# Two blocks of two feed-forward networks side by side, three of their products by quarters: seven products for eight

## The chip, the core and the metric

The kernel runs on one core of a Trainium2 chip. Its engines work in parallel: TensorE (PE, with its weight loads shown apart as PEld), VectorE (DVE), ScalarE (ACT), GpSimd (POOL) and SyncE (SP, which issues transfers). The metric is the device time of one launch in microseconds; three runs of the kernel before took 807.57, 808.49 and 808.75 us, a median of 808.49.

## What is computed

Attention over 16 heads of 768 rows (with a mask by hashed buckets), then two feed-forward networks on the 1536 rows it gives:

```python
attn_out = _attn_ref(**attn_kwargs)                       # (2, 8, 768, 64)
x = np.ascontiguousarray(attn_out.transpose(0, 2, 1, 3)).reshape(B * S, H * D)   # (1536, 512)

def _moe_ref(x, w_in, w_out):                             # w_in 512 x 2048, w_out 2048 x 512
    h = x @ w_in
    sp = np.where(h > 20.0, h, np.log1p(np.exp(np.minimum(h, 20.0))))
    return ((h * np.tanh(sp)) @ w_out).astype(np.float32)

def _moe2_ref(x, w1, w2, w3, w_out):                      # w1, w2 512 x 1024, w3 1024 x 1024, w_out 1024 x 512
    a = x @ w1
    b = x @ w2
    return ((a * b @ w3) @ w_out).astype(np.float32)
```

## The kernel before, in words

The 1536 rows are three blocks of 512 (`TB`). Block 0 goes through both networks while attention is still running for the heads of the second half (`ff_first`); blocks 1 and 2 follow when attention is done. The product of w3 and the last w_out is made once (`wprod`), so the second network is two products a and b, their elementwise product, and one more matrix product.

To reach float32 accuracy with a fast matrix format, every operand is cut in a high part and a residue (`split`, L698 on ScalarE and L700 on VectorE), and each product is three matmuls: high by high, high by residue, residue by high (`PASS`). A matmul has a 128 by 128 weight tile and up to 512 moving columns.

For blocks 1 and 2 the functions are, in the order of the work: `b_h` (one group of the first layer, 256 features: 2 halves x 4 contraction tiles x 3 passes = 24 matmuls of 512 columns on an s tile of two PSUM banks, L812 in `h_ops`; then Mish on ScalarE, L1144, and the cut into two parts, L1147 and L1149), `b_out` (the second layer, 24 matmuls of 512 columns, L1166, accumulating over all 8 groups in the four b banks), `b_x2` (cuts its result), `b_ab` (128 features of a and of b, again 24 matmuls of 512 columns on an s tile, L1193; a copy L1201, a multiplication L1202, a cut L1204 and L1205) and `b_o` (the last product, 12 matmuls a step, L1221, accumulating over 8 steps in the four b banks). Block 1 runs from its first layer to its output, then block 2; `step_list` writes out this order with a few groups of the next block moved forward. The weights are fetched from device memory for each block again (`wt`, `fetch`, L691).

The engines' orders are not written by hand. Every operation is given to `Plan.op` with its engine, an assumed cost, what it reads and writes, and a due time; `Plan.run` then plays the program forward and lets each engine take the ready operation with the earliest due time for which a buffer is free. Buffers come from pools (`Val(pool, kind, limit)`): K8 are 8 KB tiles, named k in the trace, F4 4 KB tiles, named f; PSUM has eight banks, four in two s tiles (SP_) and four b tiles (BP). Numbers in `CFG` are due times and limits. At the place called `swap` the attention's SBUF tiles are given back and the pools K8 and F4 grow.

## Time and profile before

| | us |
|---|---|
| median of 3 runs | 808.49 |
| the profiled execution, its own time | 809.2 |
| span of that execution, first to last instruction | 807.1 |
| TensorE busy | 791.4 |
| VectorE busy | 563.2 |
| ScalarE busy | 450.9 |
| GpSimd busy | 89.9 |

The span is what the instruction rows cover; the profiled execution's own time has 2.1 us more around it. Busy is the time in which at least one instruction of the engine was running by its record. A matmul's record is longer than the spacing of matmuls, because they are pipelined, so the spacing is read from starts, not from durations.

### The profile page before, as it was taken

The numbers are of one execution on the slowest core, as the hardware profiler recorded it, in microseconds if no ns is written. First come the engines' busy times: TensorE is split into PE (matmuls) and PEld (weight loads), VectorE is DVE, ScalarE is ACT, GpSimd is POOL, SyncE is SP. The second block draws the span as 40 slices with busy tenths as digits, with TensorE's granted clock in tenths as the row PEclk, the third lists the DMA queues.
The fourth block names the chain that finished last, engine by engine and source line by source line (L and its number), as shares of the span: only waits on it lengthen the run. The fifth ranks groups of instructions, "written<-read, shape, count | busy, mean of one in ns | idle before, by whom it ended". The sixth has DMA issues, their size and how long they took to land.

```text
span 807.1 us, 10733 instructions
## 1 busy us (share of the span) xinstructions
PE 791.4 (98%) x3995; PEld 621.3 (77%) x3995; DVE 563.2 (70%) x803; ACT 450.9 (56%) x724; POOL 89.9 (11%) x154
## 2 busy tenths in 40 slices
PE   8999899999999999999999999999999999999998
PEld 7667789887676777677777778888888888888886
DVE  6999799999998899999997666633733353233412
ACT  4897657668879776885774434533342254323311
POOL 4111011011221131221311100000000000000000
PEclk9999999999999999999999999999999999999999
DMA  7665446385765585847654436823122208300001
GB/s 222 206 226 184 140 140 199 95 283 162 228 232 181 199 261 169 303 146 249 176 215 163 159 108 222 300 74 96 66 79 90 94 18 321 104 27 0 1 1 52
DMA packets 42603, 124.90 MB, mean 155 GB/s; under 512 B 5156, under 2 KB 11652, under 8 KB 41528
## 3 DMA queue, kind: packets, MB, share of 16 engines
q1 hardware_dynamic: 26152, 59.08, 23.5%
q0 software_dynamic: 16256, 65.02, 22.7%
q8 instruction: 31, 0.51, 0.3%
q14 instruction: 20, 0.16, 0.1%
q10 hardware_dynamic: 144, 0.13, 0.0%
HBM read 94.37 MB, written 17.87 MB: 139 GB/s over the span
## 4 chain that ended last, share of the span: by engine, by line
PE 84%; DVE 10%; ACT 3%; issue 2%; DMA 1%; DVEq 0%; ACTq 0%; SPq 0%
PE s L1193 11%; PE b L1166 11%; PE s L812 11%; PE b L828 8%; PE b L610 6%; PE s L527 6%; PE b L581 6%; PE b L1221 5%; PE b L923 5%; PE b L812 5%; PE b L748 4%; DVE st L536 2%; PE s L471 2%; PE s L500 1%; DVE f L651 1%
## 5 line engine op out<-in xcount | busy, mean ns | idle before, releaser
L700 DVE TENSOR_TENSOR k<-f,k 128x1024 fp32r<-128x1024 f32 x96 | 115.9, 1219 | 73.7 <-ACT k L698 73.6
L539 ACT ACTIVATE E<-s,st 128x768 f32<-128x768 f32 x96 | 87.0, 906 | 37.6 <-DVE st L536 29.5
L698 ACT CAST k<-f 128x1024 fp32r<-128x1024 f32 x96 | 98.7, 1047 | 9.7 <-PE b L828 7.0
L536 DVE TENSOR_REDUCE st<-s 128x1 f32<-128x768 f32 x96 | 91.0, 950 | 9.0 <-PE s L527 8.6
L581 PE MATMUL b<-ident,E 128*128 128x128 f32 x576 | 91.9, 275 | 1.0 <-DVE k L630 0.8
L581 PEld LDWEIGHTS b<-ident,E 128*128 128x128 f32 x576 | 70.7, 140 | 27.0 <-issue 7.2
L1193 PE MATMUL s<-k,k 128*128 128x512 f32 x384 | 91.1, 393 | 0.0
L1166 PE MATMUL b<-k,k 128*128 128x512 f32 x384 | 90.0, 392 | 0.0
L812 PE MATMUL s<-k,k 128*128 128x512 f32 x384 | 90.0, 391 | 0.0
L1193 PEld LDWEIGHTS s<-k,k 128*128 128x128 f32 x384 | 72.1, 188 | 16.7
L1166 PEld LDWEIGHTS b<-k,k 128*128 128x128 f32 x384 | 72.2, 188 | 16.2
L812 PEld LDWEIGHTS s<-k,k 128*128 128x128 f32 x384 | 72.2, 188 | 15.9
L828 PE MATMUL b<-k,k 128*128 128x512 f32 x288 | 78.4, 406 | 0.8 <-ACT f L858 0.8
L828 PEld LDWEIGHTS b<-k,k 128*128 128x128 f32 x288 | 50.8, 188 | 17.5 <-issue 7.8
L610 PE MATMUL b<-T,v 128*64 128x384 f32 x288 | 62.0, 511 | 0.4 <-ACT T L405 0.3
L1202 DVE TENSOR_TENSOR f<-s,f 128x512 f32<-128x512 f32 x16 | 11.1, 692 | 69.4 <-ACT f L1201 69.4
L527 PE MATMUL s<-kb,qb 128*128 128x384 f32 x192 | 55.3, 369 | 2.3 <-DVE qa L507 1.3
L1144 ACT ACTIVATE f<-s 128x1024 f32<-128x1024 f32 x16 | 16.4, 1028 | 73.1 <-PE s L812 73.1
L748 PE MATMUL b<-k,k 128*128 128x512 f32 x192 | 53.3, 413 | 2.4 <-ACT T L405 2.0
L812 PE MATMUL b<-k,k 128*128 128x512 f32 x192 | 53.8, 408 | 0.0
L1201 ACT COPY f<-s 128x512 f32<-128x512 f32 x16 | 9.4, 587 | 76.7 <-PE s L1193 76.7
L405 ACT COPY T<-b 128x384 f32<-128x384 f32 x85 | 39.2, 479 | 20.4 <-PE b L581 19.8
(128 smaller groups left out, 1263.4 us busy)
## 6 DMA issues: line engine op xcount, KB each, us to landing
k<-in_moe_w_dram POOLq DMA_DIRECT2D x16, 1024.0 KB, 7.2
k<-in_moe_w_out_dram POOLq DMA_DIRECT2D x12, 1024.0 KB, 7.3
k<-in_moe_w_in_dram POOLq DMA_DIRECT2D x8, 1024.0 KB, 6.4
f<-keep_wi SPq DMA_DIRECT2D x16, 512.0 KB
f<-keep_wo SPq DMA_DIRECT2D x16, 512.0 KB
keep_wi<-f POOLq DMA_DIRECT2D x8, 512.0 KB, 3.7
f<-keep_wi POOLq DMA_DIRECT2D x8, 512.0 KB, 5.2
keep_wo<-f POOLq DMA_DIRECT2D x8, 512.0 KB, 4.6
```

The costliest lines, as they stand in the source:

```text
L527: nc.tensor.matmul(t()[:, a, 0:HS], lhsT=l()[0:kk, i * 128:(i + 1) * 128], rhs=r()[0:kk, a * HS:(a + 1) * HS], start=(l is qb), stop=(l is ...
L536: P.op("DVE", 0.868, lambda: nc.vector.tensor_reduce(out=s()[:, 0, i:i + 1], in_=t()[:, :, 0:HS], axis=AX.XY, op=ALU.max, negate=True), r= ...
L539: P.op("ACT", act(S, acc=True) + 0.11, lambda: nc.scalar.activation(out=e().rearrange("p (a n) -> p a n", a=2), in_=t()[:, :, 0:HS], func= ...
L581: nc.tensor.transpose(t()[:, ci * 128:(ci + 1) * 128], es[ci]()[:, kt * 128:(kt + 1) * 128], ident)
L610: nc.tensor.matmul(t()[r, 0:HS], lhsT=w, rhs=f(), start=first and j == 0, stop=last and j == CH - 1)
L698: P.op("ACT", act(1024, True), lambda: nc.scalar.copy(out=hl()[:, 0:1024], in_=f()), r=[f], w=[(hl, 0)], due=due, name="hi")
L700: P.op("DVE", dve(1024), lambda: nc.vector.tensor_sub(out=hl()[:, 1024:2048], in0=f(), in1=hl()[:, 0:1024]), r=[f, (hl, 0)], w=[(hl, 1)], ...
L748: nc.tensor.matmul(acc(), lhsT=hv()[:, ws, g_, :], rhs=wview(wo2[g_ // 2], 2)[:, rs, g_ % 2, :], start=(n == 0), stop=(n == 3 * GT - 1))
L812: nc.tensor.matmul(of(), lhsT=wview(w, KD)[:, ws, kk, (f % 2) * 128:(f % 2) * 128 + 128], rhs=kview(xhl[n][kk // 2], xs, kk), start=(m == ...
L828: nc.tensor.matmul(of(), lhsT=l(), rhs=rr(), start=(m == 0), stop=(m == len(ops) - 1))
L1166: nc.tensor.matmul(t(), lhsT=wview(w, 2)[:, ws, f, dd * 128:(dd + 1) * 128], rhs=gv[:, gs, f, :], start=(j == 0 and f == 0 and s == 0), st ...
L1193: nc.tensor.matmul(t()[:, x, :], lhsT=wview(w, KD)[:, ws, kk, (f % 2) * 128:(f % 2) * 128 + 128], rhs=kview(xx[kk // 2], xs, kk), start=(k ...
```

## The change

Blocks 1 and 2 run side by side, a group of block 2 behind the same group of block 1, so that a weight tile is fetched, cut and summed once for both (all but the second layer's, which is fetched for each). Their first layer and their pair a, b are computed by quarters. A group is a two by two arrangement: two halves of the contraction (256 each) and two halves of the outputs (128 features each, or a and b) against two halves of the 512 rows. Eight products of quarters would be needed; seven are made, of sums and differences of quarters of the weights (`sums`, L893) and of the rows (`quarters`, L828), and sums of their results (`add`, L934, and copies out of PSUM, L928 and L939) give the four output quarters. Each of the seven products is two contraction tiles by three passes: six matmuls of 256 columns (L906). Two PSUM banks of a new pool Q are used for a group, q0 and q1 in the code; the four banks of the attention's s tiles become these banks at `swap`, which now waits only for the operations that use attention's own pools. The last product of block 2 is not accumulated step by step in four banks but made at the end, one row tile of 128 rows after the other, the last one in two halves of 256 columns (`b_o_rows`).

```diff
     "lag": 1.92,
-    "prep": 11.92,
-    "wp0": 16.62,
+    "prep": 11.76,
+    "wp0": 16.6,
     "wp1": 42.29,
-    "dec0": 39.11,
-    "dec1": 130,
-    "ff0": 54.95,
-    "ff1": 106.09,
+    "dec0": 39.06,
+    "dec1": 124.72,
+    "ff0": 55.14,
+    "ff1": 118.67,
     "slack": 0.10,
     "k8": 12,
     "f4": 7,
     "hl": 3,
-    "F": 3,
+    "hl2": 6,
+    "sl": 2,
+    "lag2": 1,
+    "lag3": 1,
+    "hlk": 2,
+    "ahead": 13.19,
+    "clk": 190.46,
+    "g2": 3,
+    "F": 2,
     "cold": 8.0,
...
+    def quarters(xt, i, due, keep_):
...
+        sub(2, 1, 0, ["k0"], "t1", 0.3)
+        cut(0, ["k0", "t1"], 2 * NH_, 0.4)
+        sub(5, 4, 2, ["k1", "t1"], "t2", 0.5)
+        sub(6, 4, 1, ["k0", "k1"], "t3", 0.5)
+        sub(7, 3, 5, ["k1", "t2"], "t4", 0.6)
+        cut(1, ["k1", "t2", "t3", "t4"], 5 * NH_, 0.7)
...
+    def sums(view, due, name, r, n=128):
+
+        f, hl = Val(F4, "S", 1), Val(K8, "sl", CFG["sl"], FR)
+        sv = lambda x: f().rearrange("p (r i c) -> p r i c", r=4, i=2)[:, x]
+        for x, op, a, b in ((0, "add", (1, 0), (1, 1)), (1, "subtract", 0, (0, 0)), (2, "subtract", (0, 0), (1, 0)),
+                            (3, "subtract", (0, 1), 1)):
+            av = (lambda a=a: sv(a)) if isinstance(a, int) else (lambda a=a: view(*a))
+            bv = (lambda b=b: sv(b)) if isinstance(b, int) else (lambda b=b: view(*b))
+            rr = [(f, y) for y in (a, b) if isinstance(y, int)]
+            P.op("DVE", 0.335, lambda x=x, op=op, av=av, bv=bv: nc.vector.tensor_tensor(
+                out=sv(x), in0=av(), in1=bv(), op=getattr(ALU, op)), r=r + rr, w=[(f, x)], due=due, name=name)
+        split(f, hl, due + 0.5)
...
+    def seven(xs, wa_, ws_, r, due, step, done, name):
+
+        q0, q1, sx = Val(Q, "q"), Val(Q, "q"), Val(F4, "sx", 2)
+
+        def mm(q, c, lhs, o, first):
+            n = 0
+            for i in range(2):
+                for w, x in PASS:
+                    nc.tensor.matmul(q()[:, c * NH_:(c + 1) * NH_], lhsT=lhs(w, i), rhs=xs[i][x]()[:, qcol(o)],
+                                     start=first and n == 0, stop=n == 5, skip_group_check=True)
+                    n += 1
+
+        A = lambda m, h: (lambda w, i: wa_(m, h, w, i))
+        SS = lambda x: (lambda w, i: ws_(x, w, i))
+        g0 = [(v_, 0) for t in (0, 1) for v_ in xs[t]]
+        g1 = [(v_, 1) for t in (0, 1) for v_ in xs[t]]
+
+        def st1():
+            mm(q0, 0, A(0, 0), 0, True)
+            mm(q0, 1, SS(0), 2, False)
+
+        def st2():
+            mm(q1, 0, A(0, 1), 3, True)
+            mm(q1, 1, A(1, 1), 7, False)
+
+        def st3():
+            mm(q0, 0, SS(1), 5, False)
+            mm(q0, 1, SS(3), 4, False)
+
+        P.op("PE", 12 * 0.1185, st1, r=r + g0, w=[q0], due=due, name=name)
+        P.op("ACT", act(2 * NH_), lambda: nc.scalar.copy(out=sx()[:, 0:2 * NH_], in_=q0()), r=[q0], w=[(sx, 1)],
+             due=due + step, name="s1")
+        P.op("PE", 12 * 0.1185, st2, r=r + g1, w=[q1], due=due + step, name=name)
+        P.op("PE", 12 * 0.1185, st3, r=r + g1, w=[q0], due=due + 2 * step, name=name)
+
+        def add(o, q, c, x, w, dd):
+            P.op("DVE", dve(NH_), lambda: nc.vector.tensor_add(
+                out=done()[:, o * NH_:(o + 1) * NH_], in0=q()[:, c * NH_:(c + 1) * NH_], in1=sx()[:, x * NH_:(x + 1) * NH_]),
+                r=[q, (sx, w)], w=[(done, o)], due=due + dd * step, name="cc")
+
+        def get(x, w, dd):
+            P.op("ACT", act(NH_), lambda: nc.scalar.copy(out=sx()[:, x * NH_:(x + 1) * NH_], in_=q0()[:, 0:NH_]), r=[q0],
+                 w=[(sx, w)], due=due + dd * step, name="s2")
+
+        add(0, q1, 0, 0, 1, 2)
+        get(2, 2, 3)
+        add(1, q0, 1, 2, 2, 3)
+        P.op("PE", 6 * 0.1185, lambda: mm(q0, 0, SS(2), 6, False), r=r + g1, w=[q0], due=due + 3.5 * step, name=name)
+        get(3, 3, 4)
+        add(3, q0, 0, 1, 1, 4)
+        add(2, q1, 1, 3, 3, 4)
...
+    theirs = (SP_, EP, TP, QB, KB, QA, KA, XF, RW, HL, VP, TM, VS, RT, ST)
+    gate2 = P.op("SWAP", 0.01, swap, due=0, after=[x for x in P.units if any(v_.pool in theirs for v_ in x.vals)], name="swap")
...
+        lag, ahead = CFG["lag2"], CFG["hlk"]
+        for j in range(FP + ahead):
+            if j < FP:
+                prog.append(("h", 1, j))
+            if 0 <= j - lag < FP:
+                prog.append(("h", 2, j - lag))
+            if j == 0:
+                prog.append(("x", 2))
+            if j - ahead >= 0:
+                prog.append(("out", 1, j - ahead))
+        for j in range(FP + ahead - lag, FP):
+            prog.append(("h", 2, j))
+        prog.append(("x2", 1))
+        for j in range(FP):
+            prog.append(("out", 2, j))
+        prog += [("ab", 1, 0), ("x2", 2), ("ab", 1, 1)]
+        lag = CFG["lag3"]
+        for f in range(GT + lag + 1):
+            if 1 < f < GT:
+                prog.append(("ab", 1, f))
+            if 0 <= f - lag < GT:
+                prog.append(("ab", 2, f - lag))
+            if 0 <= f - 1 < GT:
+                prog.append(("o", 1, f - 1))
+        for t4 in range(TB // 128):
+            prog.append(("or", 2, t4))
+        return prog
...
+    def b_o_rows(n, t4):
+
+        d = clock[0]
+        last = t4 == TB // 128 - 1
+        ws = [wt("wp", n, j, d) for j in range(GT // 2)]
+        hd = DM // 2
+        cols = [slice(0, hd), slice(hd, DM)] if last else [slice(0, DM)]
+        for x, c in enumerate(cols):
+            t = Val(BP, "a")
+            for f in range(GT):
+                P.op("PE", pe(DM, 3) / len(cols), lambda t=t, f=f, c=c: o_mm(t, n, f, t4, c), r=[pp[n, f], ws[f // 2]], w=[t],
+                     due=d + 0.69 * f / len(cols) + x * 2.77, name=f"o{n}.{t4}")
+            if last:
+                o = Val(F4, "o", 4)
...
```

How the change moves instructions, at three places. Names are of tiles: q and b are PSUM banks, k and f SBUF tiles; the weights are named last; the number behind an underscore tells one use of a buffer from the next.

On TensorE, in the first layer of block 1 before: one group (L812) on bank pair s0, then a second-layer step (L1166).

```order
L812 MATMUL s0_67<-k3_2813,k2_4631 128x512 x6
L812 MATMUL s0_67<-k9_3946,k2_4631 128x512 x6
L812 MATMUL s0_67<-k3_2813,k2_4631 128x512 x6
L812 MATMUL s0_67<-k9_3946,k2_4631 128x512 x6
L1166 MATMUL b1_70<-k10_4665,k7_4644 128x512 x6
L1166 MATMUL b3_72<-k10_4665,k7_4644 128x512 x6
L1166 MATMUL b0_69<-k10_4665,k7_4644 128x512 x6
L1166 MATMUL b2_71<-k10_4665,k7_4644 128x512 x6
```

On TensorE now, in the first groups: the end of the third stage of one group (bank q2), the last six of the other group (q0), the last six of the first (q2 again), and the next group, which takes q0 over. Of each six the first is shown, and of the last two.

```order
L906 MATMUL q2_4672<-k12_4313,k1_4597 128x256
L906 MATMUL q2_4672<-k7_4216,k1_4597 128x256
L906 MATMUL q0_4633<-k6_3654,k13_4520 128x256
L906 MATMUL q0_4633<-k0_3668,k13_4520 128x256
...
L906 MATMUL q2_4672<-k6_3654,k1_4597 128x256
L906 MATMUL q2_4672<-k0_3668,k1_4597 128x256
...
L906 MATMUL q0_4766<-k17_4403,k5_4431 128x256
```

Where 24 matmuls of 512 columns stood without any read of their bank in between, banks are now read and written again within a group, with six or more matmuls of another bank in between.

On VectorE, in the stretch of a and b: before, per step a multiplication and a cut, and the residues of weight tiles (L700).

```order
L1202 TENSOR_TENSOR f_5370<-s_68,f_5370 128x512
L1205 TENSOR_TENSOR f_5379<-f_5370,f_5379 128x512
L1202 TENSOR_TENSOR f_5414<-s_67,f_5414 128x512
L1205 TENSOR_TENSOR f_5423<-f_5414,f_5423 128x512
L700 TENSOR_TENSOR k_5428<-f_5191,k_5428 128x1024
L700 TENSOR_TENSOR k_5436<-f_5199,k_5436 128x1024
```

Now, at the like place: the adds that put the quarters of the results together (L934), a sum of weight quarters (L893), the multiplication (L1358), a residue (L712) and a cut (L1361).

```order
L893 TENSOR_TENSOR f_6577<-f_6577,f_5978 128x256
L934 TENSOR_TENSOR f_6581<-q_6549,f_6562 128x256
L893 TENSOR_TENSOR f_6577<-f_5978,f_6577 128x256
L934 TENSOR_TENSOR f_6581<-q_6530,f_6562 128x256
L934 TENSOR_TENSOR f_6611<-q_6584,f_6543 128x256
L934 TENSOR_TENSOR f_6611<-q_6514,f_6543 128x256
L934 TENSOR_TENSOR f_6581<-q_6530,f_6562 128x256
L934 TENSOR_TENSOR f_6581<-q_6549,f_6562 128x256
L1358 TENSOR_TENSOR f_6581<-f_6581 128x512
L712 TENSOR_TENSOR k_6626<-f_6577,k_6626 128x1024
L1361 TENSOR_TENSOR f_6643<-f_6581,f_6643 128x512
```

The adds stand in front of the multiplication, and the work of two groups and of the weight sums is mixed in one queue.

On TensorE where attention ends, before: the last value product (L610), then 30 matmuls of L923 and 48 of L828 for block 0, then block 1 (L812).

```order
L610 MATMUL b_70<-T_4419,v_98 64x384
L923 MATMUL b_72<-k_3770,k_4367 128x512 x6
L923 MATMUL b_69<-k_3695,k_4299 128x512 x6
L923 MATMUL b_69<-k_3770,k_4299 128x512 x6
L923 MATMUL b_71<-k_3695,k_4367 128x512 x6
L923 MATMUL b_71<-k_3770,k_4367 128x512 x6
L828 MATMUL b_70<-k_4393,k_4277 128x512 x6
L828 MATMUL b_72<-k_4393,k_4277 128x512 x6
L828 MATMUL b_69<-k_4393,k_4277 128x512 x6
L828 MATMUL b_71<-k_4393,k_4277 128x512 x6
```

Now, behind the last value product (L620): 24 of L975, 48 of L1070, 24 of L975, 48 of L1070 and 48 of L975, which is 192 matmuls of block 0, and then L906.

```order
L620 MATMUL b_69<-T_4267,v_101 64x384
L975 MATMUL b_68<-k_4135,k_4092 128x512 x6
L975 MATMUL b_70<-k_4135,k_4092 128x512 x6
L975 MATMUL b_67<-k_4135,k_4092 128x512 x6
L975 MATMUL b_69<-k_4135,k_4092 128x512 x6
L1070 MATMUL b_68<-k_3958,k_4260 128x512 x6
L1070 MATMUL b_68<-k_3971,k_4260 128x512 x6
L1070 MATMUL b_70<-k_3958,k_4278 128x512 x6
L1070 MATMUL b_70<-k_3971,k_4278 128x512 x6
L1070 MATMUL b_67<-k_3958,k_4260 128x512 x6
L1070 MATMUL b_67<-k_3971,k_4260 128x512 x6
```

More of block 0 is left when attention is done, 192 matmuls for 78.

## Rows read from the trace of the kernel before

**Rows 1.** The page, busy us (share of the span) and instructions of each engine

```profile
PE 791.4 (98%) x3995; PEld 621.3 (77%) x3995; DVE 563.2 (70%) x803; ACT 450.9 (56%) x724; POOL 89.9 (11%) x154
```

**Rows 2.** Table of stretches: from:to, us, busy of each engine, granted clock, DMA

```profile
0.00:494.00 494.00, 482.16 (x2653) 369.25 (x2654) 442.33 (x672) 341.71 (x593) 89.88 (x154) 1.00 0.59 191
494.00:803.00 309.00, 309.00 (x1344) 252.03 (x1342) 120.18 (x131) 108.81 (x130) 0.00 (x0) 1.00 0.27 96
```

**Rows 3.** Chain of waits from 480 us: start, us, what

```profile
493.81 22.31 PE s L812 x96
...
521.62 5.44 PE s L812 x24
...
797.80 5.46 PE b L1221 x24
803.28 0.38 ACT f L1231
803.66 0.02 issue
803.68 0.42 DVE f L1232
```

**Rows 4.** Groups of 494 to 803 us, TensorE: count | busy us, mean ns | idle

```profile
L1193 PE MATMUL s<-k,k 128*128 128x512 f32 x384 | 91.1, 393 | 0.0
...
L812 PE MATMUL s<-k,k 128*128 128x512 f32 x384 | 90.0, 391 | 0.0
```

**Rows 5.** Timeline of TensorE at 409.5 us: start, us, what

```profile
409.45 0.34 PE L500 MATMUL s<-kb,psel 128*128 128x384 f32 x1
...
410.15 0.34 PE L500 MATMUL s<-xf,psel 128*128 128x384 f32 x1
410.33 0.86 PE L923 MATMUL b<-k,k 128*128 128x512 f32 x3
```

**Rows 6.** Timeline of TensorE at 6.6 us

```profile
6.42 0.28 PE L396 MATMUL b<-identr 128*128 128x256 f32 x1
6.54 0.29 PE L471 MATMUL s<-identr,hlqk 128*128 128x128 f32 x2
```

**Rows 7.** Timeline of TensorE at 384 us

```profile
384.10 0.71 PE L471 MATMUL s<-identr,hlqk 128*128 128x128 f32 x6
384.64 0.46 PE L828 MATMUL b<-k,k 128*128 128x512 f32 x1
```

**Rows 8.** Groups of 494 to 803 us, VectorE and ScalarE

```profile
L700 DVE TENSOR_TENSOR k<-f,k 128x1024 fp32r<-128x1024 f32 x53 | 63.6, 1221 | 71.2 <-ACT k L698 71.2
L1205 DVE TENSOR_TENSOR f<-f,f 128x512 fp32r<-128x512 f32 x16 | 11.1, 693 | 11.0 <-ACT f L1204 11.0
...
L1232 DVE COPY f<-b 128x256 f32<-128x256 f32 x1 | 0.4, 424 | 0.4 <-ACT f L1231 0.4
L698 ACT CAST k<-f 128x1024 fp32r<-128x1024 f32 x51 | 52.0, 1045 | 0.0
...
L1204 ACT CAST f<-f 128x512 fp32r<-128x512 f32 x16 | 9.9, 620 | 12.1 <-DVE f L1202 12.1
L1201 ACT COPY f<-s 128x512 f32<-128x512 f32 x16 | 9.4, 587 | 76.7 <-PE s L1193 76.7
...
L1231 ACT COPY f<-b 128x256 f32<-128x256 f32 x1 | 0.4, 372 | 3.5 <-PE b L1221 3.5
```

**Rows 9.** Table of stretches, the one with most work for VectorE (columns as in rows 2)

```profile
100.00:200.00 100.00, 97.74 (x591) 84.67 (x589) 96.97 (x160) 66.67 (x132) 15.24 (x25) 1.00 0.56 176
```

**Rows 10.** The page, transfers: KB each, us to landing

```profile
f<-keep_wi POOLq DMA_DIRECT2D x8, 512.0 KB, 5.2
```

**Rows 11.** Timeline from 802 us, the last instruction

```profile
804.14 0.37 ACTq L1234 DMA_DIRECT2D out_dram<-f  x1
```

**Rows 12.** Groups of 494 to 803 us, weight loads

```profile
L1166 PEld LDWEIGHTS b<-k,k 128*128 128x128 f32 x384 | 72.2, 188 | 16.2
```

**Rows 13.** Timeline of weight loads at 384.7 us

```profile
384.61 0.30 PEld L828 LDWEIGHTS b<-k,k 128*128 128x128 f32 x2
```

More of the change, by code (lines that the diff above doesn't have):

```diff
@@ L1151, in b_h @@
-        clock[0] += 24
+        f = raw_of[id(w)]
+        if ("h", j) not in ssum:
+            ssum["h", j] = sums(lambda m, h: quarter(f, m, h), d - AHEAD + 1, "hS", [f])
+        sw = ssum["h", j]
+        h = Val(F4, f"h{n}", 3 if n == 1 else 8)
+        seven(xq[n], lambda m, h_, s_, i: quarter(w, m, h_, s_)[:, i], lambda x, s_, i: sview(sw, x, s_, i), [w, sw], d, 1.42, h,
+              f"h{n}.{j}")
+        P.op("ACT", act(1024, True), lambda: nc.scalar.activation(out=h(), in_=h(), func=AF.Mish),
+             r=[(h, o) for o in range(4)], w=[h], due=d + ST7, name=f"mish{n}.{j}")
@@ L1198, in b_ab @@
-        p, g = Val(F4, "p", 2), Val(F4, "pg", 3, FR)
+        fa, fb = raw_of[id(wa)], raw_of[id(wb)]
+        m_ = f % 2
+        if ("ab", f) not in ssum:
+            ssum["ab", f] = sums(lambda m, h: quarter((fa, fb)[m], m_, h), d - AHEAD + 1, "abS", [fa, fb])
+        sw = ssum["ab", f]
+        p, g = Val(F4, "p", 2), Val(F4, f"pg{n}", 3 if n == 1 else 8, FR)
         pp[n, f] = g
         gv = lambda s: g().rearrange("p (s n) -> p s n", s=2)[:, s]
-        P.op("ACT", act(512), lambda: nc.scalar.copy(out=p()[:, 0:512], in_=t()[:, 0, :]), r=[(t, 0), (t, 1)], w=[p], due=d + 12, name="pa")
@@ new lines, in o_mm, with o_end @@
+    def o_mm(t, n, f, t4, c=slice(0, None)):
+        gv = pp[n, f]().rearrange("p (s n) -> p s n", s=2)
+        w = wts["wp", 0, f // 2]
+        for s, (gs, ws) in enumerate(PASS):
+            nc.tensor.matmul(
+                t()[:, c], lhsT=gv[:, gs, t4 * 128:(t4 + 1) * 128], rhs=wview(w, 2)[:, ws, f % 2, c],
+                start=(f == 0 and s == 0), stop=(f == GT - 1 and s == 2))
+    def o_end(n, t, t4, d):
+        o = Val(F4, "o", 4)
+        P.op(EITHER, (act(512), dve(512)), lambda e: copy(e, o()[:, 0:DM], t()), r=[t], w=[o], due=d, name="oe")
+        P.op("SP", 0.5, lambda: nc.sync.dma_start(out=rows_out(n, t4), in_=o()[:, 0:DM]), r=[o], due=d, name="out")
@@ L1243 @@
+    x_quarters(1, 98)
+    OPS = {"h": b_h, "out": b_out, "x2": b_x2, "ab": b_ab, "o": b_o, "or": b_o_rows, "x": lambda n: x_quarters(n, clock[0] - 10)}
     for op, *a in step_list():
```

210 lines of the change are left out of this document (111 added, 99 removed).

## The prediction

> **What bounds the kernel now.** I read the page's busy times first, then a table of stretches, then the chain of waits, and last single instructions. The busy times [rows 1] put TensorE far ahead: 791.4 of 807.1 us, VectorE at 563.2, ScalarE at 450.9. An average says nothing about the edited part, so the table of stretches [rows 2] cuts the span at 494 us, where block 1 starts: before that TensorE is idle for 11.8 us in all (494.0 less 482.16), and from there to 803 us not for a moment, while VectorE works 120.2 of 309 us and ScalarE 108.8. The granted clock is 1.00 in both stretches, the 2.4 GHz level. The chain of waits [rows 3] says the same in order of time: from 493.81 to 803.28 us it holds nothing but matmuls. So in blocks 1 and 2 the time is the number of matmuls times their spacing: (803.28 − 493.81) / 1344 = 0.2303 us for one of 512 columns. Whatever takes spacing out there shortens the kernel by as much, until something else ends last.
>
> **The sum, part by part.**
>
> *Fewer columns.* The first layer (L812 on s tiles) and the multiplied pair (L1193) of blocks 1 and 2 are 384 + 384 matmuls of 512 columns [rows 4], 32 groups of 24. They cost 768 x 0.2303 = 176.9 us. In the new kernel a group is seven products of six matmuls, each of 256 columns: 32 x 42 = 1344. The columns fall to seven eighths, but the matmuls and weight loads rise by three quarters, so everything hangs on the spacing of a 256-column matmul with a fresh weight tile. Nothing in the old trace is a run of those. Nearest are the six 384-column matmuls of L500, each with other weights: five spacings take 410.33 − 409.45 us, 0.176 each [rows 5]. From 0.176 at 384 to 0.2303 at 512 is 0.0543 for 128 columns; once more down gives 0.122 at 256. One lone 256-column matmul, a filler, stands at 6.42 us and the next starts at 6.54 [rows 6]: 0.12 as printed, with a different kind of weight load behind it. From above, six 128-column transposes with fresh weights take 0.54 us [rows 7], 0.090 each; were that overhead kept, 256 columns would cost 0.090 + 0.054 = 0.144. Between 0.117 (a little under the lone matmul) and 0.144 I take 0.122, because the 384- and 512-column rows are matmuls of the same kind, and the transposes aren't. Then 1344 x 0.122 = 164.0, a gain of **12.9 us**. Each nanosecond here is 1.3 us; the gain is gone at 176.9 / 1344 = 0.1316.
>
> The Trainium skill, in "TensorE: Matmul & The Clock Gate" (section Back-to-back issue gap), gives a warm gap of columns / 2.4 GHz plus 2.5 ns for an isolated matmul. By that the old groups would be 768 x 0.2158 = 165.7 us, the new 1344 x 0.1092 = 146.8, and the gain 18.9; the trace disagrees at 512 columns (0.2303 [rows 3]), so I hold to the rows.
>
> *Returns inside a group.* The products of a group share bank q0: ScalarE must copy it out before the third pair adds on top, and ScalarE and VectorE must read it again before the last six matmuls. The new order fills these gaps with other matmuls: at least twelve (1.46 us) between first and third stage in all 32 groups, and more than 2 us before the last six in all but two groups. In those two, and at the two reuses of a bank that follow them, only six stand (0.73 us). The reads are 0.372 us for the copy of 256 columns and 0.424 for an add of 256 [rows 8], on two engines at once. The copy on the old kernel's end starts in step with the last matmul of the chain, and the next read 0.02 us after it [rows 3], so 0.73 us just about covers one read. Four places at 0.15 us is 0.6; the bounds are 0 and, if both reads queue behind a 1.2 us subtraction [rows 8], some 4.
>
> *Work for VectorE and ScalarE.* All sums, differences and quarter cuts are new work there. The densest stretch is the multiplied pair. For one f, both blocks: eight adds and four sums of 256 columns (12 x 0.424), four 512-column operations (4 x 0.693) and two and a half 1024-column residues (2.5 x 1.221) make 10.9 us, against 84 x 0.122 + 12 x 0.2303 = 13.0 us of TensorE. VectorE is then busy 84%. I cost it at nothing, since it already runs at 97 of 100 us in another stretch [rows 9]; without that cover it is the second rival. ScalarE needs less: per f, two 512-column copies and four of 256, two of 512 and two and a half of 1024 make 2 x 0.587 + 4 x 0.372 + 2 x 0.620 + 2.5 x 1.045 = 6.5 us.
>
> *Transfers.* Weights of the first layer, the pair and the last product are now fetched once for both blocks, so SP issues fewer. A 512 KB fetch lands in 5.2 us [rows 10]; it runs some 13 us ahead by the new table, so it costs nothing. If it were late, the split and the sums behind it would be late next, by its excess.
>
> *The front, to 494 us.* The same matmuls stand there in another order: after the last attention work 192 matmuls of block 0 remain instead of 78, and they hold two banks at a time instead of three. TensorE's work is equal, so I take nothing; it can win at most part of the 11.8 us idle there (3), or lose as much.
>
> *The last rows.* The last tile's 24 matmuls of 512 become 48 of 256: 48 x 0.122 − 24 x 0.2303 = +0.3 us. At the end ScalarE and VectorE now copy one after the other, 0.38 and 0.42 us [rows 3], the last transfer is issued at 804.14 [rows 11]; with the halves in two banks the first copy is done under the second half's matmuls: −0.4 us.
>
> **The sum:** −12.9 + 0.6 + 0.3 − 0.4 = −12.4 us. The profiled execution took 809.2 us (span 807.1 and 2.1 around it), so 796.8; the median of the runs shown is 0.7 lower, 808.49, and I forecast **796.0 us**.
>
> **Rivals.**
>
> *Weight loads become the bound* (slower). One load is recorded at 0.188 us [rows 12], longer than the new matmul of 0.122. If a matmul had to wait for a whole load, the 1344 would cost 252.7 us, 75.8 more: 884. With the transposes' overhead, 0.144, they cost 193.5: 808.5 + 16.6 − 0.1 = 825. It decides from 0.1316 on. For it speaks that no run of 256-column matmuls is in the trace. Against it: two loads at 384.61 us span 0.30 us together [rows 13], so the second began 0.11 after the first, and L500's loads, also of 128 columns, went every 0.176, already less than one recorded load. I give it 6%.
> The Trainium skill's "Perfetto Trace Analysis" (Identifying the Most-Contended Engine) judges TensorE's headroom by the busy share of weight loads, and its section Matmuls prefers larger matmuls: both speak against this change, and by the first the loads would stop fitting. The pair of overlapping loads is why I give that little.
>
> *VectorE can't keep 84%.* It works in order, and each group waits for it four times. At 75% useful share one f takes 10.9 / 0.75 = 14.5 us for 13.0 of TensorE: 8 x 1.5 = 12 us back, **808**, no change; at 80% it is 13.6, 5 us back, 801. Against it is the 97% elsewhere; for it, that there the work was less tied to single matmuls. 10%: 6 near 802, 3 at 808, 1 above.
>
> *The front gets longer.* In the 192 matmuls behind attention, a bank of six (1.38 us) is emptied by a VectorE add of 0.69, while VectorE also makes block 1's quarters. If each of the 16 such banks of L975 waits 0.35 us, that is 5.6 us: 802. 8%.
>
> *Nothing changes in the bound but the spacing is better*, 0.117: 157.2 us, 6.7 us more gain, and 2 from the front: **787**. 10%.
>
> **How the numbers follow.** The forecast, 0.118 to 0.126 and small waits, holds 66% and spans 791 to 803. Range: down to 787 for the better spacing; up to 805, which takes in the front and the VectorE case at 80%; the load case and VectorE's worst lie outside. A measurement of this kernel can tell 0.2% (1.6 us) from no change. Faster: 66 + 10 + 8 + 6 = 90%. Same: 3%, from VectorE at 75%. Slower: 7%, the loads and a worse VectorE.
>
> **What would show it.** In the new profile, L906's spacing: 42 matmuls in 5.1 us (0.122) with nothing of other engines between. If a spacing is over 0.13 with the engine never idle, the loads have it; if TensorE's idle time ends on VectorE lines L934 or L712, the second rival. The first L906 should start near 494 us, later means the front. TensorE's stretch from there to its last matmul should be about 1344 x 0.122 + 552 x 0.2303 + 48 x 0.122 = 297 us. The forecast is wrong if the whole is under 787 or over 805.

## The result, and the profile after

The changed kernel takes 793.58 us (median of 4 runs, 792.99 to 794.73) against 808.3 us for the kernel before on the same chip (4 runs): a ratio of 0.982, with a 95% interval of 0.9803 to 0.9838. The forecast was 796.0 us in a range of 787 to 805. The profiled execution took 793.2 us with a span of 791.4; before, 809.2 and 807.1. The spans differ by 15.7 us, the medians by 14.7, mostly because the profiled execution before was 0.9 us above its median. One of the ten executions of the kernel with eight products (first experiment) ran at a granted clock of 0.85 and took 867.7 us; it is left out, and since it is the profiled one, no trace of that kernel is used.

The page, busy times of each engine (as in [rows 1]):

```profile
PE 775.5 (98%) x4594; PEld 637.4 (81%) x4594; DVE 641.7 (81%) x1020; ACT 490.0 (62%) x811; POOL 85.3 (11%) x154
```

TensorE still bounds the kernel: 599 more matmuls are recorded, and it is 15.9 us less busy. VectorE has 78.5 us more work and is busy 81% of a shorter span.

The table of stretches, with the columns of [rows 2], cut where the first L906 begins (495 us), at block 2's second layer alone (612 to 664), at the pair a, b (664 to 765) and at the last product alone:

```profile
0.00:495.00 495.00, 483.15 (x2650) 368.77 (x2651) 453.57 (x696) 351.75 (x605) 85.26 (x154) 1.00 0.61 195
495.00:515.00 20.00, 19.45 (x163) 19.12 (x162) 16.26 (x31) 12.25 (x19) 0.00 (x0) 1.00 0.40 133
515.00:612.00 97.00, 97.00 (x672) 90.20 (x671) 58.21 (x98) 54.50 (x79) 0.00 (x0) 1.00 0.24 77
612.00:664.00 52.00, 52.00 (x232) 42.99 (x231) 38.06 (x53) 25.61 (x30) 0.00 (x0) 1.00 0.23 71
664.00:765.00 101.00, 100.78 (x763) 96.57 (x763) 70.48 (x135) 44.33 (x79) 0.00 (x0) 1.00 0.07 24
765.00:788.10 23.10, 23.09 (x124) 19.71 (x122) 4.73 (x9) 1.58 (x3) 0.00 (x0) 1.00 0.21 78
```

The granted clock is 1.00 throughout. TensorE idles 11.85 us in the front, as before (494.0 less 482.16 [rows 2]), and less than a microsecond from 495 to 788 us. In a and b, which I had taken for the densest stretch, VectorE works 70.5 of 101 us: 70%. It is denser in block 2's second layer (38.1 of 52 us, 73%) and in the first 20 us (16.3 of 20, 81%). Those 20 us hold 0.55 us of TensorE's idle time, the most of any stretch behind 495 us.

The chain of waits of the changed kernel (start, us, what), the pieces that give a spacing:

```profile
557.49 9.20 PE q L906 x78
...
588.53 9.21 PE q L906 x78
...
611.71 51.93 PE b L1327 x228
...
694.51 9.22 PE q L906 x78
...
765.07 23.03 PE b L1369 x123
```

A 256-column matmul with a fresh weight tile comes every 9.21 / 78 = 0.1181 us, one of 512 columns, in the long piece of the second layer, every 51.93 / 228 = 0.2278. Over all pieces the second layer's 384 matmuls take 88.0 us, 0.2292 each (0.2303 before, as a mean over all lines [rows 3]). The last line holds 75 matmuls of 512 columns and 48 of 256; at 0.2303 for the long ones, the short ones went every 0.120.

Groups on TensorE and VectorE in the changed kernel (count | busy us, mean ns | idle before and what ended it):

```profile
L906 PEld LDWEIGHTS q<-k,k 128*128 128x128 f32 x1344 | 163.5, 189 | 4.0 <-DVE f L934 1.2
L906 PE MATMUL q<-k,k 128*128 128x256 f32 x1344 | 164.7, 281 | 0.8 <-DVE f L934 0.8
L934 DVE TENSOR_TENSOR f<-q,f 128x256 f32<-128x256 f32 x128 | 51.6, 421 | 59.4 <-ACT f L939 39.6
```

What TensorE waited for at L906 in the whole run (us in total, times, longest):

```profile
PE q L906 <- DVE f L934: 0.8, 2, 0.6
```

The recorded weight load is still 0.19 us long, longer than the 0.119 between matmuls that each have one: consecutive loads overlap. The adds L934, the likeliest late step, made TensorE wait 0.8 us in all.

Where the 15.7 us of the span come from, in the terms of the prediction:

| term | forecast | measured |
|---|---|---|
| 1344 matmuls of 256 columns for 768 of 512 | −12.9 | −17.2 (1344 x 0.1188 − 176.9) |
| returns inside a group (idle at L906) | +0.6 | +0.8 |
| second layer, 384 x (0.2292 − 0.2303) | 0 | −0.4 |
| last product, its last tile in halves (44.5 − 192 x 0.2303) | +0.3 | +0.3 |
| front (first matmul of block 1: 493.8 to 495.1 us) | 0 | +1.3 |
| tail (last matmul to end: 3.8 to 3.3 us) | −0.4 | −0.5 |
| sum | −12.4 | −15.7 |

The 0.1188 is what is left of the stretch 495.1 to 788.1 us without the idle time (0.8), the second layer (88.0) and the last product (44.5, both sums of their pieces of the chain), divided by 1344; the long pieces of the chain give 0.118.

### The profile page after: what moved, and what is told of

Read it like the earlier page. It is cut to its first block, busy times and chain, and to the rows that moved or that the text cites. A ratio compares the mean times of both kernels' runs of the same rounds, so it can differ in the third digit from the quotient of the medians.

```text
span 791.4 us, 12290 instructions
## 1 busy us (share of the span) xinstructions
PE 775.5 (98%) x4594; PEld 637.4 (81%) x4594; DVE 641.7 (81%) x1020; ACT 490.0 (62%) x811; POOL 85.3 (11%) x154
## 4 chain that ended last, share of the span: by engine, by line
PE 83%; DVE 10%; ACT 4%; issue 2%; DMA 1%; ACTq 0%; DVEq 0%; SPq 0%
PE q L906 19%; PE b L1327 11%; PE b L975 7%; PE b L620 7%; PE s L537 6%; PE b L1070 6%; PE b L591 6%; PE b L1369 6%; PE b L760 5%; PE b L959 4%; DVE st L546 2%; PE s L481 2%; PE s L510 2%; PE b L406 1%; DMA v<-in_v_dram 1%
## 5 line engine op out<-in xcount | busy, mean ns | idle before, releaser
L906 PEld LDWEIGHTS q<-k,k 128*128 128x128 f32 x1344 | 163.5, 189 | 4.0 <-DVE f L934 1.2
L906 PE MATMUL q<-k,k 128*128 128x256 f32 x1344 | 164.7, 281 | 0.8 <-DVE f L934 0.8
L712 DVE TENSOR_TENSOR k<-f,k 128x1024 fp32r<-128x1024 f32 x92 | 111.6, 1223 | 12.8 <-ACT k L710 12.6
L710 ACT CAST k<-f 128x1024 fp32r<-128x1024 f32 x92 | 95.2, 1050 | 34.9 <-PE b L975 9.3
L934 DVE TENSOR_TENSOR f<-q,f 128x256 f32<-128x256 f32 x128 | 51.6, 421 | 59.4 <-ACT f L939 39.6
L1327 PE MATMUL b<-k,k 128*128 128x512 f32 x384 | 90.6, 391 | 0.0
L975 PE MATMUL b<-k,k 128*128 128x512 f32 x288 | 77.6, 405 | 0.8 <-DVE k L640 0.8
L975 PEld LDWEIGHTS b<-k,k 128*128 128x128 f32 x288 | 51.2, 188 | 19.0 <-issue 8.4
L939 ACT COPY f<-q 128x256 f32<-128x256 f32 x64 | 23.8, 371 | 68.7 <-PE q L906 66.2
L620 PE MATMUL b<-T,v 128*64 128x384 f32 x288 | 63.1, 511 | 0.0
L959 PE MATMUL b<-k,k 128*128 128x512 f32 x192 | 55.8, 413 | 0.0
L415 ACT COPY T<-b 128x384 f32<-128x384 f32 x91 | 41.9, 479 | 20.5 <-PE b L591 19.2
L760 PE MATMUL b<-k,k 128*128 128x512 f32 x192 | 51.5, 402 | 2.9 <-ACT T L415 2.5
L537 PE MATMUL s<-ka,qa 76*128 76x384 f32 x192 | 49.6, 339 | 0.0
L1070 PE MATMUL b<-k,k 128*128 128x512 f32 x192 | 49.0, 400 | 0.5 <-ACT T L415 0.5
L1369 PE MATMUL b<-k,f 128*128 128x512 f32 (+1 forms) x216 | 47.1, 368 | 0.0
```

The source lines that it names most:

```text
L537: nc.tensor.matmul(t()[:, a, 0:HS], lhsT=l()[0:kk, i * 128:(i + 1) * 128], rhs=r()[0:kk, a * HS:(a + 1) * HS], start=(l is qb), stop=(l is ...
L620: nc.tensor.matmul(t()[r, 0:HS], lhsT=w, rhs=f(), start=first and j == 0, stop=last and j == CH - 1)
L710: P.op("ACT", act(1024, True), lambda: nc.scalar.copy(out=hl()[:, 0:1024], in_=f()), r=[f], w=[(hl, 0)], due=due, name="hi")
L712: P.op("DVE", dve(1024), lambda: nc.vector.tensor_sub(out=hl()[:, 1024:2048], in0=f(), in1=hl()[:, 0:1024]), r=[f, (hl, 0)], w=[(hl, 1)], ...
L760: nc.tensor.matmul(acc(), lhsT=hv()[:, ws, g_, :], rhs=wview(wo2[g_ // 2], 2)[:, rs, g_ % 2, :], start=(n == 0), stop=(n == 3 * GT - 1))
L906: nc.tensor.matmul(q()[:, c * NH_:(c + 1) * NH_], lhsT=lhs(w, i), rhs=xs[i][x]()[:, qcol(o)], start=first and n == 0, stop=n == 5, skip_gr ...
```

## Experiments

Unless said otherwise each kernel is the changed one with one edit, and ratios are to the kernel before.

**Eight products instead of seven.** Side by side as in the change, but 24 matmuls of 512 columns a group, without sums or adds.

```diff
+    def eight(xs, wa_, r, due, step, done, name):
...
+        for m, q in enumerate((q0, q1)):
+            for h in range(2):
...
+                        for w, x in PASS:
+                            nc.tensor.matmul(q(), lhsT=wa_(m, h, w, i), rhs=xs[i][x]()[:, KCOL[h]],
...
```

> The changed kernel with eight products for seven: a group is again 24 matmuls of 512 columns, two q banks per group, no sums and differences; block order, shared weights, q banks and last rows stay as changed. Theory A (the gain is the columns: 768 x 0.2303 us against 1344 x 0.1188 as the changed kernel's trace has it): 17.2 us back, less at most 0.6 for the one wait at the start, so 810 us (808 to 812), no faster than the kernel before. Rival B (the gain comes from the order, blocks side by side, weights fetched and cut once): most of it stays, 800 us or less.

Measured: 810.02 us (median of nine runs), ratio 1.0024 (1.0014 to 1.0033). Blocks side by side with shared fetches and cuts gain nothing by themselves. The seven products are worth 16.4 us against this kernel (810.02 on one chip, 793.58 on another); the columns less the idle time at L906 make 17.2 − 0.8 = 16.4 by the table above. So the gain is the columns that seven products for eight take out, and the order of the work only has to leave them free: the later experiments show orders that do not.

**The same products at 128 columns.** Each 256-column matmul is issued as two of 128, each with its own weight load.

```diff
-                    nc.tensor.matmul(q()[:, c * NH_:(c + 1) * NH_], lhsT=lhs(w, i), rhs=xs[i][x]()[:, qcol(o)],
+                    for y in range(2):
+                        nc.tensor.matmul(q()[:, c * NH_ + y * 128:c * NH_ + (y + 1) * 128], lhsT=lhs(w, i),
...
```

> The changed kernel with each 256-column matmul of the seven products issued as two of 128 columns on the same weight tile: the same columns, 2688 matmuls and weight loads for 1344. It asks how near the weight load is to setting the spacing. Theory A (columns plus a small constant: the line through 0.2288 at 512 and 0.1188 at 256 gives 0.064 at 128): 172 us for 160, so 806 us. Rival B (a load can follow a load every 0.108 us at best, as the pair in the old trace): spacing 0.108 to 0.112, 290 to 301 us, so 924 to 935 us. Rival C (the pace of the 128-column transposes, 0.085 to 0.090): 228 to 242 us, 862 to 876 us.

Measured: 933.77 us, ratio 1.1555 (1.1534 to 1.1576). Its chain of waits shows the spacing directly:

```profile
495.86 36.13 PE q L907 x324
```

36.13 / 324 = 0.1115 us for 128 columns. Half the columns took only 6% off the spacing of 0.1181. Columns no longer set the pace there, so what is left is something that each matmul with its load costs, about 0.11 us. That it is the load is argued, since no run issued two of these matmuls on one load: the two loads of [rows 13] started 0.11 us apart beside matmuls of 512 columns, while the transposes, of 128 columns too, came every 0.090 us [rows 7] with loads of a shorter record, 140 ns for 188 [rows 12]:

```profile
L471 PEld LDWEIGHTS s<-identr,hlqk 128*128 128x128 f32 x192 | 18.8, 140 | 7.5 <-ACT qb L477 2.9 <-ACT E L539 1.0 <-ACT f L642 0.6
```

This is the first rival of the prediction, true at 128 columns and just not at 256: the new matmul sits 6% above the weight-load pace. The Trainium skill, "TensorE: Matmul & The Clock Gate" (section LDWEIGHTS (loading the stationary operand)), gives columns / 1.2 GHz for a load, 107 ns for 128; this run agrees within 5%, while the load's record, 192 ns here, does not show it. The same page (section Back-to-back issue gap) has about 81 ns for a sustained 128-column matmul; here it was 112.

**The adds made twice.** Every L934 is issued two times with the same operands, 128 more adds of 0.42 us on VectorE.

```diff
-            P.op("DVE", dve(NH_), lambda: nc.vector.tensor_add(
...
+            def twice():
+                for _ in range(2):
+                    nc.vector.tensor_add(
...
+            P.op("DVE", 2 * dve(NH_), twice,
```

> The changed kernel with every add that puts the quarters of results together (L934) done twice: 128 more adds of 256 columns on VectorE, 54 us of records, 27 of them in the stretch of a and b, where VectorE then has some 97 us of records in 101. Theory A (VectorE's work is hidden behind TensorE with room): 793 to 797 us. Rival B (VectorE is useful for 75% of the time at most when every group waits for it): the a and b stretch grows to 97 / 0.75 = 130 us, so some 820 us.

Measured: 801.19 us, ratio 0.9915 (0.9901 to 0.9928), between the two theories. Table of stretches of this kernel (first groups; first layer; a and b):

```profile
496.20:516.00 19.80, 17.64 (x133) 17.27 (x132) 17.70 (x37) 10.71 (x16) 0.00 (x0) 0.91 0.39 129
516.00:616.20 100.20, 100.20 (x699) 93.39 (x698) 80.92 (x154) 56.03 (x81) 0.00 (x0) 1.00 0.23 75
...
668.20:773.40 105.20, 103.08 (x766) 96.81 (x766) 94.68 (x198) 45.12 (x79) 0.00 (x0) 1.00 0.07 23
```

TensorE's wait at L906 in it:

```profile
PE q L906 <- DVE f L936: 3.7, 5, 1.7
```

The 54 us of extra VectorE work cost 7.6 us. At 90% busy (94.7 of 105.2) VectorE made the stretch of a and b 4.2 us longer than at 70%; of the rest, 3.0 us lie in the first groups and the first layer, and 1.1 ahead of the first L906. In the first layer VectorE was busy 81% (80.9 of 100.2 us) and TensorE had no idle time. So my second rival is real at 90%, and neither the 70% of a and b in the changed kernel nor this 81% brings it on; where between it begins was not measured.

**The last product step by step.** Block 2's last product accumulates in four banks again, as before the change.

```diff
-        for t4 in range(TB // 128):
-            prog.append(("or", 2, t4))
+        for f in range(GT):
+            prog.append(("o", 2, f))
```

> The changed kernel with the last product of block 2 accumulated step by step in four banks, as before, instead of row tile by row tile. Theory A (the row tiles only shorten the very end): the last copy is of 512 columns (0.69 us for 0.42) and the last transfer twice as large, 24 matmuls of 512 for 48 of 256 (0.2 us less): 0.1 to 0.8 us more, 793.7 to 794.4 us, not to be told from no change. Rival B (the four copies and transfers queue at the end): 2 to 4 us more, 796 to 798 us.

Measured: 793.98 us, ratio 0.9825 (0.9812 to 0.9838), the first theory. By the medians the row-tile order is worth 0.4 us, which the intervals can't tell from nothing; in the traces the time from the last matmul to the end is 4.0 us here and 3.3 in the changed kernel.

**Each block fetches, cuts and sums its own weights**, still side by side: 71 us more work for VectorE.

```diff
-        key = (nm, n if nm == "wo" else 0, j)
+        key = (nm, n, j)
...
-        if ("h", j) not in ssum:
-            ssum["h", j] = sums(lambda m, h: quarter(f, m, h), d - AHEAD + 1, "hS", [f])
+        if ("h", n, j) not in ssum:
+            ssum["h", n, j] = sums(lambda m, h: quarter(f, m, h), d - AHEAD + 1, "hS", [f])
```

> The changed kernel, blocks side by side and seven products, but each block fetches, cuts and sums its own weights (as before for the fetches): 20 more residues and 16 more sets of sums on VectorE, 20 x 1.22 + 16 x (4 x 0.42 + 1.22) = 71 us of records more. Theory A (sharing matters, because VectorE is the next bound): in the stretch of a and b VectorE has 70.5 + 38 = 108 us of records for 101 of TensorE, so 10 to 20 us more, 803 to 814 us. Rival B (VectorE has room, sharing saves only transfers that are hidden): 793 to 797 us.

Measured: 799.6 us, ratio 0.9898 (0.9885 to 0.9912), short of the first theory's loss and beyond the second's. Table of stretches of this kernel (first groups; a and b):

```profile
496.10:519.00 22.90, 20.54 (x160) 20.34 (x159) 22.74 (x43) 17.34 (x24) 0.00 (x0) 0.93 0.46 161
...
668.60:773.60 105.00, 103.55 (x773) 98.55 (x772) 99.42 (x187) 63.89 (x101) 0.00 (x0) 1.00 0.27 84
```

TensorE's wait at L906 in it:

```profile
PE q L906 <- DVE f L934: 3.8, 3, 2.4
```

VectorE is busy 22.7 of 22.9 us where the blocks begin, and 95% in a and b, which takes 105.0 us for 101. With the adds made twice it took 105.2, so the same loss comes with extra work that is not in the adds. Sharing the weights is worth 6 us. The largest wait at L906 ends on VectorE; ScalarE's casts and the fetches, doubled with it, were not tried apart.

**Block after block.** Seven products, but block 1 to its end before block 2, each with its own weights, and the last product step by step.

```diff
+        for n in (1, 2):
+            first = 0 if n == 1 else 2
+            for j in range(first, FP + 2):
+                if j < FP:
+                    prog.append(("h", n, j))
...
-        key = (nm, n if nm == "wo" else 0, j)
+        key = (nm, n, j)
...
```

> Seven products, but block after block as before: each block fetches, cuts and sums its own weights, the last product of block 2 is accumulated step by step. Theory A (the order side by side is what lets the work on VectorE hide): the 71 us more on VectorE, and nothing of TensorE's stands between the second layer of block 2 and its a and b, where the quarters of 512 columns by 512 take some 7 us: 805 to 818 us, little or nothing left of the gain. Rival B (only the number of columns counts): 793 to 797 us.

Measured: 803.75 us, ratio 0.9944 (0.9929 to 0.9959), a little better than the first theory's range and far from the second's. What TensorE waited for in this kernel, the two lines of L906:

```profile
PE q L906 <- DVE f L934: 3.3, 4, 0.9
PE q L906 <- DVE k L839: 3.0, 3, 1.1
```

Without a second block's matmuls to fill in, TensorE waits for adds in more places, and for the quarters of the second network's rows (L839), which nothing covers. Block after block, seven products still beat eight, by 3.9 us (803.75 against 807.62 for the kernel before on the same chip); side by side, shared weights and the row tiles bring the other 10 (803.75 against 793.58).

**The front values of before.** The change also moved seven numbers that time the work ahead of 495 us. Here all seven are as before, in the changed kernel.

```diff
-    "prep": 11.76,
-    "wp0": 16.6,
+    "prep": 11.92,
+    "wp0": 16.62,
...
-    "dec0": 39.06,
-    "dec1": 124.72,
-    "ff0": 55.14,
-    "ff1": 118.67,
+    "dec0": 39.11,
+    "dec1": 130,
+    "ff0": 54.95,
+    "ff1": 106.09,
...
-    "F": 2,
+    "F": 3,
```

> The changed kernel with the due times and the bank limit of the front as before (prep, wp0, dec0, dec1, ff0, ff1, F = 3). In the changed kernel's trace the first matmul of the quarters stands at 495.1 us, 1.3 later than block 1's first before. Theory A (the moved due times cost that): it starts near 494 us and the time is 792.3 us, 1.3 less. Rival B (block 0's rest and block 1's quarters now meet on VectorE whatever the due times, more so with less of block 0 left as cover): 795 us or more.

Measured: 810.87 us, ratio 1.0036 (1.0024 to 1.0049). The whole gain is gone. The first L906 starts at 511.1 us instead of 495.1, and from there to the last matmul the kernel takes 293.8 us, against 293.0: only the front differs. Table of stretches of this kernel, the last two ahead of L906:

```profile
440.00:480.00 40.00, 33.63 (x129) 26.65 (x130) 37.26 (x53) 19.85 (x25) 7.94 (x13) 0.88 0.77 270
480.00:511.00 31.00, 31.00 (x135) 25.11 (x134) 25.87 (x37) 15.42 (x19) 0.00 (x0) 1.00 0.20 75
```

The largest wait of TensorE in it:

```profile
PE b L1070 <- DVE k L712: 9.2, 2, 4.8
```

TensorE stands at block 0's pair (L1070) and waits for residues (L712) of w1 and w2, while VectorE is busy 93%. Ahead of its first L906 it is idle for 25.1 us, where it was 11.85 in the changed kernel: 13.2 of the 16 us. Most of the rest is clock. Behind the first of the two waits, of 4.8 us, ten matmuls of 512 columns take 4.4 us instead of 2.3, at half the clock, the 1.2 GHz level (table of stretches of this kernel):

```profile
442.00:446.40 4.40, 4.40 (x10) 3.47 (x11) 2.45 (x4) 3.27 (x3) 2.02 (x3) 0.50 0.97 361
```

The residues come late because the weights do. Before w1 and w2 can be used their raw form is loaded (L668), decoded by VectorE, stored and fetched again. GpSimd issues these transfers one after the other, and in this kernel it waits in front of one of those loads from 392.6 to 418.5 us:

```profile
418.47 0.76 POOL L668 DMA_DIRECT2D k<-in_moe_w_dram  x1 [25.83 <-PE b L1070]
```

The load writes a k tile, and the profile has the wait end on a matmul of block 0 (L1070). The next five runs ask why.

**One front value of before alone.**

```diff
-    "ff1": 118.67,
+    "ff1": 106.09,
```

> The changed kernel with one front value of before: the due time step ff1 of block 0's work behind attention, 106.09 instead of 118.67. With all front values of before the first L906 came at 511.1 us instead of 495.1 and the whole took 810.9. Theory A: the late start came from the last weight tiles, whose decodes waited for buffers that block 1's quarters of x took too early; with ff1 alone the quarters move earlier against those decodes, so most of the 16 us comes back: first L906 at 505 to 511, 803 to 811 us, and TensorE waits for VectorE's L712 by several us. Theory B: ff1 is not the one that matters (dec1 or F is): first L906 at 494 to 498, 792 to 797 us.

Measured: 815.33 us, ratio 1.0093 (1.0079 to 1.0107), worse than all seven together and than either theory. The first L906 starts at 517.5 us. TensorE's largest wait in this kernel:

```profile
PE b L1070 <- ACT k L710: 10.7, 1, 10.7
```

The wait is at the same place, now for ScalarE's part of the same cut, which waits for a fetch: the last two loads L668 are issued only at 456.7 and 457.5 us here. The values act together; one taken from another setting is no half step towards it.

**The kernel before with the new front values**, the same seven numbers the other way round.

```diff
-    "ff1": 106.09,
+    "ff1": 118.67,
...
```

> The kernel before with the front values of the changed kernel. Theory A: the new values only make up for what the new blocks put into the front, so the old kernel gets nothing from them: 805 to 811 us, within 0.4% of before. Theory B: the values are a gain of their own that would come without the seven products: 795 to 803 us.

Measured: 809.13 us, ratio 1.0019 (1.001 to 1.0028): the first theory. The numbers are worth 17 us (810.87 against 793.58) in the new code and −1.5 us in the old.

**The front values of before, with block 1's quarters held back** behind the load of the last weight decode.

```diff
...
-    x_quarters(1, 98)
+    x_quarters(1, 98, [x for x in P.units if x.name == "wb3l"])
```

> The front values of before in the changed kernel, as in the run with all seven values, but block 1's quarters of x are held back behind the load of the last weight decode. Theory A: the quarters took the 8 KB tiles that the last decodes needed; held back, the decodes come in time: first L906 at 494 to 499, 791 to 798 us. Theory B: the tiles are not the cause (the order of the work on VectorE is): first L906 stays at 507 or later, 806 to 812 us.

Measured: 808.29 us, ratio 1.0005 (0.9996 to 1.0014). The first L906 is early, at 497.4 us, as the first theory said, and the time is the second's. The stretch behind it (table of stretches of this kernel) shows why:

```profile
495.00:515.00 20.00, 12.62 (x78) 11.25 (x77) 20.00 (x35) 8.66 (x11) 0.00 (x0) 0.83 0.63 210
```

TensorE's waits at L906 in it:

```profile
PE q L906 <- DVE k L712: 4.5, 2, 3.0
PE q L906 <- ACT k L710: 2.9, 1, 2.9
PE q L906 <- DVE f L934: 2.6, 3, 2.0
```

Block 0's weights come in time now, and block 1's are late: VectorE works 20.0 of 20 us and TensorE 12.6. The wait was moved, not removed.

The front itself is answered by this run. With the quarters held back the last load L668 is issued at 421.2 us instead of 443.4 (422.3 in the changed kernel), GpSimd does not wait in front of any of the five loads from 389.4 us on, and the first L906 comes 13.7 of the 16 us earlier. So with these front values it was block 1's early quarters that held back the last decodes. That they did it by the 8 KB tiles they took, as the first theory says, fits the wait shown above, but no run changed the number of tiles alone.

**The same gate in the changed kernel**, with its own front values.

> The changed kernel with its own front values, and block 1's quarters of x held back behind the load of the last weight decode. Theory A: in the changed kernel the values already put the quarters late enough, so this changes nothing: 792 to 796 us. Theory B: some of the front's remaining idle time (12 us before the first L906) still comes from the same tiles: 788 to 791.5 us. Theory C: held back, the quarters come too late for block 1's first products: TensorE waits for VectorE's L870 at the first L906, 796 to 803 us.

Measured: 799.87 us, ratio 0.99 (0.9886 to 0.9913), the third theory's time by another mechanism: the first L906 starts at 500.5 us, and the largest wait in front of it is again at block 0's pair (waits of this kernel):

```profile
PE b L1070 <- DVE k L712: 2.8, 2, 1.9
```

Here the same gate moved the last load L668 the other way, to 438.8 us from 422.3: what holding back the quarters does depends on the order around it.

**The front values of before with less work for VectorE**, in the same order on every engine: the corrections of x in the quarters work on 32 columns.

```diff
-                        out=rb()[:, s0:s1], in0=rb()[:, s0:s1], scalar1=TINY, scalar2=mvs[:, b * KD + kk:b * KD + kk + 1],
+                        out=rb()[:, s0:s0 + 32], in0=rb()[:, s0:s0 + 32], scalar1=TINY, scalar2=mvs[:, b * KD + kk:b * KD + kk + 1],
...
-                P.op("DVE", dve(TB), lambda rb=rb, xd=xd: nc.vector.tensor_add(out=xd(), in0=xd(), in1=rb()),
+                P.op("DVE", dve(TB), lambda rb=rb, xd=xd: nc.vector.tensor_add(out=xd()[:, 0:32], in0=xd()[:, 0:32], in1=rb()[:, 0:32]),
```

> The changed kernel with all seven front values of before, in the same order on every engine, but the corrections of x in the quarters of blocks 1 and 2 (L875 and L880) work on 32 columns instead of 256 or 512: the values of x are then not the reference's. That takes about 5 us of VectorE's work out between 405 and 476 us (L875 3.1 and L880 4.0 in all, less what short ones still cost). Theory A: what delays the last weights there is VectorE, which works through the quarters and the decodes in one order and is 93% busy from 440 to 480 us: first L906 from 511.1 to 505 to 508, the whole 804.5 to 808 us. Theory B: the delay is in the loads, whose tiles come free late: first L906 at 510 to 512, 809.5 to 812 us.

Measured: 807.95 us, ratio 1.0004 (0.9993 to 1.0015), against 1.0036 with the full corrections: 2.6 us of 808 less. The first L906 moved from 511.1 to 509.0 us, between the theories. The stretch of this kernel that answers to the first of the run with the full corrections:

```profile
440.00:480.00 40.00, 36.30 (x138) 28.85 (x139) 34.30 (x53) 20.57 (x27) 7.94 (x13) 0.87 0.84 295
```

Its largest wait of TensorE:

```profile
PE b L1070 <- DVE k L712: 6.6, 2, 3.9
```

From 400 to 480 us L875 and L880 now take 2.7 us instead of 7.2, so 4.5 us less work brought the first L906 2.1 us forward and cut the wait from 9.2 to 6.6 us. VectorE is part of the delay. The last load of w1 and w2 to be decoded is issued at 443.9 us, against 443.4 with the full corrections and 422.3 in the changed kernel: that part did not move, and neither did GpSimd's wait in front of these loads:

```profile
418.40 0.76 POOL L668 DMA_DIRECT2D k<-in_moe_w_dram  x1 [26.06 <-PE b L1070]
```

VectorE's work is not what makes the loads late; holding back the quarters, two runs above, is what moved them.

## Why the prediction was right, point by point

- **What bounds the kernel**: right. TensorE is idle for under 1 us from 495 to 788 us, and the time is matmuls times spacing. The run with eight products shows that the gain is the columns.
- **The spacing at 256 columns** was the term that was mis-sized. I took 0.122 from a straight line through 512 and 384 columns; it is 0.1188, near the lone filler's 0.12 [rows 6] and the low bound of 0.117. That alone made the gain 4.3 us larger, 17.2 for 12.9, where the whole sum missed by 3.3. Why the line came out high is not shown; a bound by weight loads would have made the spacing longer than the line gave, not shorter, and their pace, 0.1115, lies below. The transposes [rows 7], my upper bound, were no guide, since they cost less than a product matmul of the same 128 columns (0.090 against 0.1115).
- **Weight loads become the bound**: wrong at 256 columns, right at 128. I gave the right reason (two loads 0.11 us apart [rows 13]); the run at 128 columns measured the same 0.11. The margin at 256 columns is 6%, which I did not see, since I set the limit by price (0.1316) and not by pace.
- **VectorE at 84% in a and b, costed at nothing**: no cost, but the share was 70%, and it was not the densest stretch. Part of the weight cuts and sums that I counted per step are done in earlier stretches: 12 cuts of L712 and 20 sums of L893 stand in that stretch, where I counted 20 and 32. So the changed kernel never tried the 84% that I costed at nothing. The runs with doubled adds and with own weights show the cost that I feared, 4 us of that stretch at 90 to 95%, less than the 5 to 12 us I had for 80 and 75%.
- **Returns inside a group**: +0.6 forecast, 0.8 us measured, at the line that I named: 0.55 us at 505.0 us and 0.22 at 673.1, in the first groups of the first layer and of the pair. I had four places at 0.15. In the first of them the add stands behind a residue (L712) of 1.2 us on VectorE, the case that I had as the upper bound.
- **The front, "I take nothing"**: right in the sum, +1.3 us, and by luck. I argued from equal work on TensorE and read past the seven changed due times. VectorE is the tight one there. Its busy time from 440 us to block 1's first matmul, in the kernel before:

```profile
440.00:494.00 54.00, 54.00 (x259) 39.41 (x258) 38.45 (x56) 23.28 (x37) 3.06 (x5) 1.00 0.32 109
```

The changed kernel:

```profile
440.00:495.00 55.00, 55.00 (x248) 43.21 (x247) 48.27 (x73) 27.00 (x35) 3.76 (x6) 1.00 0.43 156
```

It rises from 38.5 of 54 us to 48.3 of 55 us, mostly because of quarters of the rows (L828, L839, L870, L875, L880) and weight sums (L893), which take 17.5 us there. With the old due times the same code loses 16 to 17 us in the front, three times my third rival's price of 5.6 us, and not at L975's banks, where I put it, but at L1070's weights, which were loaded late because block 1's quarters were early. The fewer columns make the gain, and the changed kernel keeps it because the order of its front was fitted to the new load.
- **The tail**: −0.4 forecast, −0.5 measured. The last product's order itself, taken back alone, made no difference that can be told.

What stays open: by what block 1's early quarters hold the last loads back with the old front values. Held back, they give 13.7 of the 16 us, and less of their work on VectorE gives 2; that the rest is the tiles they occupy is likely by the 25.8 us wait for a tile, and not shown by itself. With the new front values the same gate made the last load later, and why was not followed up. No version that was run beats the changed kernel.

## What to carry to other kernels

Where TensorE never waits, a product made with fewer columns pays even with more and shorter matmuls, as long as each takes longer than the pace of fresh weight tiles: here 0.11 us for each, which 256 columns (0.119) just clear and 128 do not. Take the pace of weight loads from the starts of consecutive loads, never from the length of one record. The additions that buy such a saving land on another engine; size them for each stretch, the one before the new work included, since there they cost nothing in one order and 16 to 17 us in another. Buffers belong to that sizing: work that is done early holds its tiles early, and a load that other work waits for can be behind it.

## What was not expected of the hardware

- A product matmul of 128 columns with a fresh weight tile comes every 0.1115 us, one of 256 every 0.118 to 0.119, one of 512 every 0.229: the second 128 columns cost 0.007 us, the next 256 another 0.110.
- VectorE could run at 90 to 95% of a 105 us stretch, tied to single groups of six matmuls, and cost that stretch only 4 us.
- Of the schedule and not of the chip: one due time lower by 12.6 (ff1) changed the time by 22 us (815.3 against 793.6), with the same operations in another order.
- Where TensorE waited for some microseconds at a time, the granted clock of the stretch was lower: 0.83 with 7.4 of 20 us idle (quarters held back), 0.91 with 2.2 of 19.8 (adds made twice), and 0.50 for the ten matmuls behind a wait of 4.8 us (front values of before). Such a wait also slows the matmuls behind it, to 0.44 us each for 0.23 in that last case. It is not so behind every idle time: the stretch of a and b with the adds made twice had 2.1 us idle of 105.2 at 1.00. The changed kernel's own stretches are all at 1.00.
